# Nine elementwise instructions between SBUF tiles issued on GpSimd instead of VectorE, in a one-core attention and FFT kernel

## The chip, the cores and the metric

The kernel runs on one core of one Trainium2 chip. The metric is device time in microseconds (us) of one execution, the median of several runs. Five engines take part: TensorE (PE in the profile; its weight loads are PEld), VectorE (DVE), ScalarE (ACT), GpSimd (POOL) and SyncE (SP, which here only issues transfers). Each engine runs its own instructions strictly in the order in which they stand in the program, and waits on semaphores for the others.

## The reference

Two branches read the same input `x` (1 x 2048 x 448) and are mixed by a gate for each token:

```python
g = _sigmoid((x * gate_w).sum(-1, keepdims=True))
a = _A_ref(x, A_wqkv, A_wo)      # 16 heads of 28, softmax attention over 2048 tokens, output projection
b = _B_ref(x, B_w_r, B_w_i)      # irfft2(rfft2(x) * (w_r + 1j * w_i)) over tokens and channels
return g * a + (1 - g) * b
```

## The kernel before

**Attention.** Heads are worked on in four groups `g` of four (one head for each 32-partition strip), queries in four columns `c` of 512. That gives 16 group-column pairs, numbered `n`: the first eight are groups 0 and 1, the last eight groups 2 and 3. For each pair PE makes the scores of 16 key tiles (L500, `ps<-q,k`). The exponential of most key tiles is taken on ACT (L1111, into the ring buffer `ring`, 1024 columns at a time). For two to five key tiles of each pair it is approximated without ACT: DVE adds a constant to the scores, clamps them and writes them as 16-bit integers whose bits are a bf16 number (L1061, `pd<-ps`), and GpSimd makes three shifted copies of each such tile with one 64-bit integer addition a copy (L1075, `INT64_ADD pd<-pd`). The four versions of a tile, each with its own value weights `vd`, are summed on PE (L500, `pvb<-pd,vd`) together with the ACT tiles (`pvb<-ring,vw`). There are nine `pd` buffers, so GpSimd cannot write a copy before PE has read the one that lay in its buffer.

**Projections.** `proj_group` projects q and k of a group: DVE scales the product out of PSUM into `q` or `k` (L804), squares it (L809, `sq<-q` or `sq<-k`, four instructions of 128 x 512 for q of group 1), PE sums the squares (`ps<-sq,cst`), DVE copies the sums out (L826, `nrow`) and SP writes them as an extra row into `q` or `k`.

**Normalising.** At the end of each pair `n`, `normalise` copies the sums out of PSUM (L1241, `pvs`), sends the denominators through DRAM and back, broadcast (`rs`, `rr`, `Rb`), and multiplies `pvs` by `Rb` into `q` (L1253).

**FFT.** `background` runs the spectral branch between the attention's instructions: a transform over channels (16 steps `fwd`), over tokens (`fwd2`), then 16 steps `mid`, numbered `g`, which multiply the spectrum by the complex weights (L1437, products `t12` and `t34` out of PSUM), form the real and the imaginary part from them (L1442 subtracts, L1444 adds, both 128 x 225, SBUF to SBUF, into `Z`), and transform back on PE (`ps<-Z,CS`).

**Order.** Nothing is scheduled at run time. A table in the file (`TABLE`) gives the order in which every operation is emitted and the PSUM bank that it uses, so each engine's order is fixed by it. A DVE instruction that is marked `lk=True` goes through `ported`: the GpSimd instruction that follows it in the emitted order is given a wait for it (`self.port` in `pin`), so that the two do not run side by side. The squares, the multiplication of `normalise` and both `Z` instructions are so marked.

Of the kernel before, what the change touches and what calls it, by code (L numbers as in the profile page):

```python
# [19 lines left out]
ALU = mybir.AluOpType  # L20
# [123 lines left out]
def rows_of(ap, row0, stride, count, dims, offset=0):  # L144
    pitch = ap.ap[0][0]
    return _AP(tensor=ap.tensor, offset=ap.offset + row0 * pitch + offset,
               ap=[[pitch * stride, count]] + [list(d) for d in dims])
# [10 lines left out]
def dv(n, rate=1):  # L158
    return 0.067 + n / 960.0 / rate
# [145 lines left out]
class Kernel:  # L305
# [54 lines left out]
    def passed(self, ins):  # L360
        o = self.sc.op_now
        if o is None:
            return
        if o.eng == "PE":
            self.npe += 1
            for d in o.deps:
                if d.name == "dexp":
                    for p in d.all:
                        self.taken.setdefault(p.name, self.npe)
            o.at = self.npe  # L370
        elif o.name in ("dp1", "dexp"):
            o.at = max([d.at for d in o.deps if d.eng == "PE" or d.name == "dp1"])
            if self.copies:
                self.tc.declare_no_dep(ins, group="dexp", reason="product done",
                                       keep=[p for p in self.copies if self.taken.get(p.name, o.at) >= o.at])
            if o.name == "dexp":
                self.tc.add_to_no_dep_group("dexp", ins)
                self.copies.append(ins)
        o.all.append(ins)
# [409 lines left out]
    def proj_group(self, w, g, blocks, due, rel):  # L789
        self.sc.ctx = ("proj_group", w, g, tuple(blocks))  # L790
        nc = self.nc
        T = (self.k if w == "k" else self.q)[g]
        e2s, e1s = [], []
        prev = list(self.sqmm)
        nb = len(blocks)
        for j, b in enumerate(blocks):
            it = Item()
            dd = due - 8 + 5.0 * (j + 1) / nb
            m = self.proj_mms(w, g, b, it, dd, rel)
            dst = T[:, 512 * b:512 * b + 512]  # L800
            sqs = self.sq[:, 512 * b:512 * b + 512]

            def f1(dst=dst, it=it):
                self.pin(nc.vector.tensor_scalar(out=dst, in0=self.bgi(it), scalar1=SQ, scalar2=None,  # L804
                                                 op0=ALU.mult))
            e1 = self.dve(dv(512), f1, (m, ("kwar", g) if w == "k" else None), dd - 1.5, free=it)

            def f2(dst=dst, sqs=sqs):
                self.pin(nc.vector.tensor_tensor(out=sqs, in0=dst, in1=dst, op=ALU.mult))  # L809
            e2s.append(self.dve(dv(512, 2), f2, [e1] + prev, dd, lk=True))  # L810
            e1s.append(e1)
        it = Item()
        ms = []

        def f3():
            for j, b in enumerate(blocks):
                self.mm(self.bgi(it)[32 * j:32 * j + 32, :], self.c("sel4"), self.sq[:, 512 * b:512 * b + 512],
                        True, True, tile_position=(0, 32 * j))
        ms.append(self.pe(512, f3, e2s + [self.d_cst2], due - 3, mode="col", acq=it))
        self.sqall = getattr(self, "sqall", []) + ms  # L820
        self.sqmm = self.sqmm[:2] + [ms[-1]]
        self.nrow_i = getattr(self, "nrow_i", -1) + 1
        nr = self.nrow[self.nrow_i % 2]

        def f4():
            self.pin(nc.vector.tensor_copy(out=nr[0:32 * nb, :], in_=self.bgi(it)[0:32 * nb, :]))  # L826
        users = self.__dict__.setdefault("nrow_u%d" % (self.nrow_i % 2), [])
        ev = self.dve(dv(512), f4, [ms[-1]] + users, due - 3, free=it)
        row = 1 if w == "k" else 0
        ds = []  # L830
        for j, b in enumerate(blocks):
            def o(b=b):
                return rows_of(T[:], row, 32, 4, [[1, 512]], 512 * b)

            def i(j=j):
                return rows_of(nr[:], 32 * j, 1, 4, [[1, 512]])
            ds.append(self.dma(o, i, [ev] + e1s + e2s, due - 2.5, dur=0.55, lat=2.2))
        for b in blocks:
            (self.kev if w == "k" else self.qev)[g, b] = ds + e1s
        users[:] = ds  # L840
        if w == "k":
            self.knr[g, blocks[0]] = (nr, ev, users)
# [354 lines left out]
    def normalise(self, n, last):  # L1197
        self.sc.ctx = ("normalise", n)
        nc, sc = self.nc, self.sc
        g, c = self.groups[n]  # L1200
        i = n % 2
# [3 lines left out]
        pvs, rs, rr = self.pvs[i], self.rs[i], self.rr[i]  # L1205
        dst = self.q[g][:, 512 * c:512 * c + 512]
        if n == 15:
            kk = -50.0
# [31 lines left out]
        kk = t0 + 4  # L1240
# [7 lines left out]
        def bc(s):  # L1248
            src = sc_[:]
            return _AP(tensor=src.tensor, offset=src.offset + 512 * s, ap=[[0, 32], [1, 512]])  # L1250
        ds = [self.dma(lambda s=s: self.Rb[32 * s:32 * s + 32, :], lambda s=s: bc(s), (d2, self.rblast), kk, lat=2.5)
              for s in range(4)]
        e = self.dve(dv(512), lambda: self.pin(nc.vector.tensor_tensor(out=dst, in0=pvs[:], in1=self.Rb[:], op=ALU.mult)),  # L1253
                     ds, kk, lk=True)
        self.nlast[i] = self.rblast = e
        self.onorm[g, c] = e
        if g == 3:
# [73 lines left out]
    def background(self):  # L1331
        nc, sc = self.nc, self.sc
# [11 lines left out]
        def due(c):  # L1344
            return t_a + (t_b - t_a) * c / total
# [56 lines left out]
        pr, prw, prz, prt = [None, None], [None, None], [[], []], [None, None]  # L1402
# [6 lines left out]
        for g in range(NT):  # L1409
            i = g % 2  # L1410
            sc.ctx = ("mid", g)
            cost += 1.63
            k = due(cost)
            Wg, t12, t34, Z, CS = self.Wg[i], self.t12[i], self.t34[i], self.Z[i], self.CSt[i]
# [21 lines left out]
            def prod(out, it, Wg, off):  # L1436
                self.pin(nc.vector.tensor_tensor(out=out[:], in0=self.bgi(it)[:, 0:F2].rearrange("p (a f) -> p a f", a=2),  # L1437
                                                 in1=free_dims(Wg[:], [[F, 2], [1, F]], off), op=ALU.mult))
            o1 = self.dve(.54, lambda a=(t12, it, Wg, F): prod(*a), ops[-1:] + dl[1:] + prz[i], k)
            o2 = self.dve(.54, lambda a=(t34, it, Wg, 0): prod(*a), [o1] + prz[i], k, free=it)  # L1440
            prw[i] = o2
            z1 = self.dve(dv(225, 2), lambda t12=t12, Z=Z: self.pin(nc.vector.tensor_tensor(  # L1442
                out=Z[:, 0, :], in0=t12[:, 0, :], in1=t12[:, 1, :], op=ALU.subtract)), [o1, prt[i]], k, lk=True)
            z2 = self.dve(dv(225, 2), lambda t34=t34, Z=Z: self.pin(nc.vector.tensor_tensor(  # L1444
                out=Z[:, 1, :], in0=t34[:, 0, :], in1=t34[:, 1, :], op=ALU.add)), [o2, prt[i]], k, lk=True)
            prz[i] = [z1, z2]
            it2 = Item()
            ops2 = []
# [28 lines left out]
        for t in range(NT):  # L1477
            sc.ctx = ("inv", t)
            cost += .61
            k = due(cost)  # L1480
            v2 = self.V2[t % 3]
            d = self.dma(lambda v2=v2: v2[:], lambda t=t: rows_of(self.UT[:], 32 * (t >> 2) + (t & 3), 4, 8,
                                                                  [[F4, NT], [1, F4]]), vev + [v2r[t % 3]], k - 4, lat=3.5)
# [62 lines left out]
```

## Time and profile before

| | |
|---|---|
| Median of 3 runs | 380.87 us (379.72 to 381.80) |
| The profiled execution, its own time | 380.92 us |
| Its span, first to last instruction | 379.0 us |
| DVE busy | 336.6 us (89%) in 649 instructions |

The span is the part of the execution between the first and the last instruction of the program, so 1.9 us of the execution lie around it. Busy times of different engines overlap and do not add up to the span. A group's row gives the line in the program, the engine, the operation, the tiles written and read with their shapes, the count, then busy time, the mean of one in ns, and the engine's idle time just before these instructions, with what ended it. The granted TensorE clock was full throughout (0.999 of it as the mean).

### The profile page before, as it was taken

To read this page: it belongs to the slowest core of one execution; us is meant where nothing else is said; L and a number is where in the kernel's file an instruction comes from. 1 tells how busy PE (TensorE), PEld (TensorE's weight loads), DVE (VectorE), ACT (ScalarE), POOL (GpSimd) and SP (SyncE) were. 2 spreads that over 40 slices of the span, in tenths; PEclk is the share of its full clock that TensorE was granted. 3 is DMA by queue.
4 is the path that set the end of the run, shared out by engine and by line. 5 is a ranking of instruction groups with operands and counts; after the bars stand their busy time and mean duration, and the time that the engine had idled before them with its cause. 6 is when DMAs were issued, how large, how long until landed. Compare 5 with 4: busy or idle time off the path is not lost.

```text
span 379.0 us, 12133 instructions
## 1 busy us (share of the span) xinstructions
PE 367.8 (97%) x5093; PEld 144.0 (38%) x5093; DVE 336.6 (89%) x649; ACT 350.6 (92%) x389; POOL 234.9 (62%) x264
## 2 busy tenths in 40 slices
PE   8999999999999999999999999999999989999995
PEld 5644233343333332334334434233333333433563
DVE  1769889999999999999999999999999989996644
ACT  2799999999999999999989999999999999999741
POOL 4707295747878876483463556877877759654610
PEclk9999999999999999999999999999999999999999
DMA  6601001001201122113211212212313222222122
GB/s 145 171 3 45 3 5 47 21 6 39 60 15 31 47 57 52 51 38 99 68 38 39 70 36 73 59 39 64 80 41 80 66 48 80 70 67 72 48 78 88
DMA packets 31154, 21.20 MB, mean 56 GB/s; under 512 B 16260, under 2 KB 29052, under 8 KB 31100
## 3 DMA queue, kind: packets, MB, share of 16 engines
q1 hardware_dynamic: 29708, 19.96, 20.0%
q8 instruction: 40, 0.66, 0.7%
q10 hardware_dynamic: 1392, 0.46, 0.5%
q14 instruction: 14, 0.11, 0.1%
HBM read 14.51 MB, written 1.96 MB: 43 GB/s over the span
## 4 chain that ended last, share of the span: by engine, by line
PE 49%; ACT 41%; DVE 5%; SPq 1%; issue 1%; DMA 1%; POOL 0%; DVEq 0%; POOLq 0%
ACT ring L1111 41%; PE ps L500 32%; PE pvb L500 16%; DVE pd L1061 3%; SPq L475 1%; PE ps L503 1%; DMA out_dram<-wpk 1%; DVE X L1373 0%; DVE pvs L1241 0%; DVE t L1437 0%; DMA Wg<-in_B_w_r_dram 0%; ACT V L1321 0%; DVE wpq L1299 0%; DVE wpk L1299 0%; DVE Ab L1390 0%
## 5 line engine op out<-in xcount | busy, mean ns | idle before, releaser
L1111 ACT ACTIVATE ring<-ps 128x1024 bf16<-128x1024 f32 x374 | 345.6, 1135 | 7.3 <-PE ps L500 7.1
L1075 POOL INT64_ADD pd<-pd x207 | 213.0, 1044 | 107.2 <-DVE pd L1061 32.3
L1061 DVE TENSOR_SCALAR pd<-ps 128x512 uint16<-128x512 f32 x260 | 177.2, 715 | 6.1 <-PE ps L500 3.8
L500 PE MATMUL ps<-q,k 32*128 32x512 bf16 x1024 | 143.7, 382 | 4.3 <-ACT ring L1111 1.5
L500 PE MATMUL pvb<-pd,vd 128*32 128x512 bf16 x1104 | 94.8, 384 | 0.0
L500 PEld LDWEIGHTS <-k 32*128 32x128 bf16 x1024 | 40.9, 91 | 118.1 <-issue 113.2
L500 PE MATMUL pvb<-ring,vw 128*32 128x512 bf16 x748 | 68.8, 384 | 0.4 <-DVE pvs L1241 0.4
L500 PEld LDWEIGHTS <-vd 128*32 128x32 bf16 x1104 | 24.3, 95 | 33.1 <-issue 27.8
L500 PEld LDWEIGHTS <-vw 128*32 128x32 bf16 x748 | 17.5, 94 | 25.3 <-issue 22.4
L500 PEld LDWEIGHTS <-xT 128*128 128x128 bf16 (+5 forms) x512 | 19.4, 97 | 10.8 <-issue 9.9
L1437 DVE TENSOR_TENSOR t<-ps,Wg 128x450 bf16<-128x450 f32 x32 | 19.0, 619 | 1.5 <-PE pvb L500 1.0
L500 PE MATMUL ps<-xT,wpq 128*32 128x512 bf16 (+3 forms) x248 | 19.4, 382 | 0.3 <-DVE wpq L590 0.3
L500 PE MATMUL ps<-xT,wpk 128*32 128x512 bf16 (+3 forms) x244 | 18.4, 383 | 0.0
L1373 DVE TENSOR_TENSOR X<-ps,oc 128x226 bf16<-128x226 f32 (+1 forms) x32 | 12.2, 385 | 0.6
L500 PE MATMUL ps<-wvr,xT 128*128 128x112 bf16 (+1 forms) x192 | 12.7, 213 | 0.0
L500 PEld LDWEIGHTS <-CS 128*32 128x32 bf16 x384 | 8.8, 95 | 9.5 <-issue 5.2
L804 DVE TENSOR_SCALAR q<-ps 128x512 bf16<-128x512 f32 x15 | 10.3, 684 | 2.3 <-PE ps L500 2.3
L500 PE MATMUL ps<-wpk,q 128*32 128x448 bf16 x128 | 11.7, 362 | 0.0
L500 PE MATMUL ps<-wpq,q 128*32 128x448 bf16 x128 | 11.5, 362 | 0.0
L500 PE MATMUL ps<-Bd,xT 128*32 128x226 bf16 (+2 forms) x256 | 11.1, 263 | 0.3 <-ACT ring L1111 0.3
L1494 DVE TENSOR_TENSOR X<-ps,ogb 113x512 bf16<-113x512 f32 x16 | 10.3, 674 | 1.2 <-PE ps L500 1.2
L804 DVE TENSOR_SCALAR k<-ps 128x512 bf16<-128x512 f32 x15 | 10.3, 684 | 0.9 <-PE ps L500 0.8
(99 smaller groups left out, 270.5 us busy)
## 6 DMA issues: line engine op xcount, KB each, us to landing
Rb<-rsc SPq DMA_DIRECT2D x60, 64.0 KB
CS<-cCS SPq DMA_DIRECT2D x16, 192.0 KB
V<-xtok SPq DMA_DIRECT2D x16, 113.0 KB
Wg<-in_B_w_i_dram SPq DMA_DIRECT2D x64, 28.1 KB
xtok<-Ab SPq DMA_DIRECT2D x16, 112.5 KB
xtok<-in_A_x_dram SPq DMA_DIRECT2D x3, 448.0 KB
Wg<-in_B_w_r_dram SPq DMA_DIRECT2D x32, 28.1 KB
out_dram<-wpq SPq DMA_DIRECT2D x6, 112.0 KB
```

Of the source, the lines that this page charges most:

```text
L475: self.pin(e.dma_start(out=out() if callable(out) else out, in_=in_() if callable(in_) else in_))
L500: self.pin(self.nc.tensor.matmul(out, lhsT=lhsT, rhs=rhs, start=start, stop=stop, **kw))
L503: self.pin(self.nc.tensor.transpose(out=out, in_=in_, identity=self.c("ident")[0:n, 0:n]))
L804: self.pin(nc.vector.tensor_scalar(out=dst, in0=self.bgi(it), scalar1=SQ, scalar2=None, op0=ALU.mult))
L1061: self.pin(nc.vector.tensor_scalar(out=free_dims(ys[:], [[512 * e, w], [1, 512]], 512 * part[0]).bitcast(U16), in0=self.ps[:, bs[0]:bs[0] ...
L1075: self.pin(nc.gpsimd.int64_add(out=fl(pds), in0=fl(ys), in1=PHASE[f] * 0x0001000100010001))
L1111: self.pin(nc.scalar.activation(out=self.ring[:, u0:u0 + len(st), :], in_=self.ps[:, bs[0]:bs[0] + len(st), :], func=ACT.Exp, scale=LN2 / ...
L1373: self.pin(nc.vector.tensor_tensor(out=free_dims(self.X1[:, t, :], [[F, 2], [-1 if dif else 1, n]], (F - 1) * dif), in0=free_dims(self.bgi ...
L1437: self.pin(nc.vector.tensor_tensor(out=out[:], in0=self.bgi(it)[:, 0:F2].rearrange("p (a f) -> p a f", a=2), in1=free_dims(Wg[:], [[F, 2], ...
L1494: self.pin(nc.vector.tensor_tensor(out=free_dims(self.zt[0:FN], [[128, 4], [1, 128]], 512 * t), in0=self.bgi(it)[0:FN, :].rearrange("p (a ...
```

## The change

Nine instructions move from DVE to GpSimd (`nc.vector.tensor_tensor` becomes `nc.gpsimd.tensor_tensor`), at the same place of the emitted order: the four squares of q of group 1, the multiplication in `normalise` of the pair n = 3, and the subtraction and addition of the `mid` steps 5 and 6. As GpSimd instructions they are not marked `lk`. One line of bookkeeping in `passed` keeps a dependency on the instruction just before on the same engine. No loop, table entry, bank or tile changes.

```diff
@@ passed
-                                       keep=[p for p in self.copies if self.taken.get(p.name, o.at) >= o.at])
+                                       keep=[p for p in self.copies
+                                             if p is self.before.get(ins.engine) or self.taken.get(p.name, o.at) >= o.at])
@@ proj_group
-                self.pin(nc.vector.tensor_tensor(out=sqs, in0=dst, in1=dst, op=ALU.mult))
-            e2s.append(self.dve(dv(512, 2), f2, [e1] + prev, dd, lk=True))
+                e = nc.gpsimd if (w, g) == ("q", 1) else nc.vector
+                self.pin(e.tensor_tensor(out=sqs, in0=dst, in1=dst, op=ALU.mult))
+            e2s.append(self.pool(0.6, f2, [e1] + prev, dd) if (w, g) == ("q", 1) else
+                       self.dve(dv(512, 2), f2, [e1] + prev, dd, lk=True))
@@ normalise
+        if n == 3:
+            e = self.pool(0.9, lambda: self.pin(nc.gpsimd.tensor_tensor(out=dst, in0=pvs[:], in1=self.Rb[:], op=ALU.mult)),
+                          ds, kk)
+        else:
...
@@ background
+            ze, zn = (nc.gpsimd, lambda d, f, p: self.pool(d, f, p, k)) if g in (5, 6) else \
+                (nc.vector, lambda d, f, p: self.dve(d, f, p, k, lk=True))
+            z1 = zn(dv(225, 2), lambda t12=t12, Z=Z, ze=ze: self.pin(ze.tensor_tensor(
+                out=Z[:, 0, :], in0=t12[:, 0, :], in1=t12[:, 1, :], op=ALU.subtract)), [o1, prt[i]])
+            z2 = zn(dv(225, 2), lambda t34=t34, Z=Z, ze=ze: self.pin(ze.tensor_tensor(
+                out=Z[:, 1, :], in0=t34[:, 0, :], in1=t34[:, 1, :], op=ALU.add)), [o2, prt[i]])
```

The order in which the instructions of GpSimd stand around the squares, before. A row that begins with `L1075 ISA pd` is one `INT64_ADD`; the number behind a name is that of the buffer, and the brackets name the semaphores that the instruction waits for:

```order
L888 COPY vt<-w_89 128x20 [waits DVE_49,Activation_49]
L1075 ISA pd_110<-pd_108 128x1024
L1075 ISA pd_108<-pd_107 128x1024 [waits DVE_49,Pool_49]
L1075 ISA pd_105<-pd_103 128x1024
L1075 ISA pd_109<-pd_107 128x1024 [waits PE_49]
L1075 ISA pd_110<-pd_107 128x1024 [waits PE_49]
L1075 ISA pd_105<-pd_111 128x1024 [waits DVE_49,PE_49]
```

The same place of the change (its line numbers are a few higher: L1078 for L1075, L811 for L809):

```order
L811 ISA
L811 TENSOR_TENSOR sq<-q_81 128x512
L811 TENSOR_TENSOR sq<-q_81 128x512 [waits DVE_49] x2
L891 COPY vt<-w_89 128x20 [waits Activation_49]
L1078 ISA
L1078 ISA pd_110<-pd_108 128x1024
L1078 ISA pd_108<-pd_107 128x1024 [waits DVE_49,Pool_49]
L1078 ISA pd_105<-pd_103 128x1024
L1078 ISA pd_109<-pd_107 128x1024 [waits PE_49]
L1078 ISA pd_110<-pd_107 128x1024 [waits PE_49]
L811 ISA
L811 TENSOR_TENSOR sq<-q_81 128x512 [waits DVE_49]
```

The next row is again an `ISA` without operands, and then the additions go on. Such a row loads another library of GpSimd programs (it is a `PseudoReloadLibraryIndex` in the built program): index 0 ahead of a `TENSOR_TENSOR`, index 1 ahead of an `INT64_ADD`, since the two operations are in different libraries. The program before has one such row in all, ahead of its first `INT64_ADD`; the change has eleven. So what moved here is four squares and, with them, four library changes; and the wait of the `vt` copy for DVE is gone.

Further on in GpSimd's order, around the `Z` instructions of the `mid` steps 5 and 6, before:

```order
L1075 ISA pd_109<-pd_107 128x1024 [waits PE_49]
L1075 ISA pd_108<-pd_106 128x1024 [waits DVE_49,PE_49]
L888 COPY vt<-w_91 128x20
L1075 ISA pd_104<-pd_111 128x1024 [waits DVE_49]
L1075 ISA pd_105<-pd_111 128x1024
L1075 ISA pd_103<-pd_111 128x1024 [waits PE_49]
L1075 ISA pd_109<-pd_106 128x1024 [waits PE_49]
L1075 ISA pd_107<-pd_106 128x1024
L1075 ISA pd_104<-pd_110 128x1024 [waits DVE_49,PE_49]
```

The same place of the change, up to the second pair of `Z`:

```order
L1078 ISA pd_109<-pd_107 128x1024 [waits PE_49]
L1453 ISA
L1453 TENSOR_TENSOR Z_145<-t_143 128x225 [waits DVE_49]
L1451 TENSOR_TENSOR Z_145<-t_141 128x225 [waits DVE_49]
L1078 ISA
L1078 ISA pd_108<-pd_106 128x1024 [waits PE_49]
L891 COPY vt<-w_91 128x20
L1078 ISA pd_104<-pd_111 128x1024 [waits DVE_49]
L1078 ISA pd_105<-pd_111 128x1024
L1078 ISA pd_103<-pd_111 128x1024 [waits PE_49]
L1078 ISA pd_109<-pd_106 128x1024 [waits PE_49]
L1078 ISA pd_107<-pd_106 128x1024
```

Behind the last of these rows, ahead of `pd_104<-pd_110`, stands the second pair of `Z`, again between two library changes. The multiplication of `normalise` stands alone in the same way, with a change on both sides: it comes behind the third memset of an output weight (L728), ahead of `pd_111<-pd_109`. That makes five places with two library changes each. On DVE the nine rows are gone and nothing else moves; the orders of PE, ACT and SP are the same as before, with some of their waits turned from DVE to GpSimd.

More of the change, by code (lines that the diff above doesn't have):

```diff
@@ L1252, in normalise @@
               for s in range(4)]
-        e = self.dve(dv(512), lambda: self.pin(nc.vector.tensor_tensor(out=dst, in0=pvs[:], in1=self.Rb[:], op=ALU.mult)),
-                     ds, kk, lk=True)
+        if n == 3:
+            e = self.pool(0.9, lambda: self.pin(nc.gpsimd.tensor_tensor(out=dst, in0=pvs[:], in1=self.Rb[:], op=ALU.mult)),
+                          ds, kk)
+        else:
+            e = self.dve(dv(512), lambda: self.pin(nc.vector.tensor_tensor(out=dst, in0=pvs[:], in1=self.Rb[:], op=ALU.mult)),
+                         ds, kk, lk=True)
         self.nlast[i] = self.rblast = e
@@ L1441, in background @@
             prw[i] = o2
[L1442 to L1445, printed above, removed]
+            ze, zn = (nc.gpsimd, lambda d, f, p: self.pool(d, f, p, k)) if g in (5, 6) else \
[4 more added lines that the diff above has]
+                out=Z[:, 1, :], in0=t34[:, 0, :], in1=t34[:, 1, :], op=ALU.add)), [o2, prt[i]])
             prz[i] = [z1, z2]
```

## The prediction

> **What bounds the kernel now.** I read the page's busy times first, then the chain of work that ended last, then the timelines of ACT and of POOL.
>
> ```profile
> PE 367.8 (97%) x5093; PEld 144.0 (38%) x5093; DVE 336.6 (89%) x649; ACT 350.6 (92%) x389; POOL 234.9 (62%) x264
> PE 49%; ACT 41%; DVE 5%; SPq 1%; issue 1%; DMA 1%; POOL 0%; DVEq 0%; POOLq 0%
> ```
>
> The chain is made of PE and ACT; DVE, which the change relieves, holds 5% of it. POOL, which takes the work, has 38% of the span idle and no part in the chain. The shares are averages, so the places have to be looked at. ACT in order of time (start, duration, then what; the bracket is idle time just before):
>
> ```profile
> 82.13 81.10 ACT L1111 ACTIVATE ring<-ps 128x1024 bf16<-128x1024 f32 x88
> 163.41 5.61 ACT L1111 ACTIVATE ring<-ps 128x1024 bf16<-128x1024 f32 x6 [0.18 <-PE ps L500]
> 169.30 1.94 ACT L1111 ACTIVATE ring<-ps 128x1024 bf16<-128x1024 f32 x2 [0.28 <-PE ps L500]
> ...
> 185.39 8.36 ACT L1111 ACTIVATE ring<-ps 128x1024 bf16<-128x1024 f32 x9 [0.17 <-PE ps L500]
> 194.29 1.94 ACT L1111 ACTIVATE ring<-ps 128x1024 bf16<-128x1024 f32 x2 [0.55 <-PE ps L500]
> 196.87 4.82 ACT L1111 ACTIVATE ring<-ps 128x1024 bf16<-128x1024 f32 x5 [0.64 <-PE ps L500]
> ...
> 201.84 109.24 ACT L1111 ACTIVATE ring<-ps 128x1024 bf16<-128x1024 f32 x119
> 311.37 39.70 ACT L1111 ACTIVATE ring<-ps 128x1024 bf16<-128x1024 f32 x43 [0.29 <-PE ps L500]
> ```
>
> From 82 us to 351 us ACT does exponentials one behind the other. Its marked gaps there are 0.18 + 0.28 + 0.17 + 0.55 + 0.64 + 0.29 = 2.1 us. Whatever DVE is spared in this stretch, no more than these 2.1 us can come out of it; and every microsecond for which ACT is made to stand still is added to the end.
>
> PE is as full, as five stretches around the changed places show (the columns are the stretch and its length, then the busy time of PE, PEld, DVE, ACT and POOL, each with its count of instructions, the clock, DMA share and GB/s):
>
> ```profile
> 80.00:90.00 10.00, 9.72 (x143) 4.49 (x140) 8.96 (x21) 10.00 (x13) 7.03 (x8) 1.00 0.16 37
> 90.00:100.00 10.00, 10.00 (x145) 3.13 (x142) 9.96 (x19) 10.00 (x12) 8.65 (x9) 1.00 0.10 28
> 140.00:150.00 10.00, 10.00 (x154) 3.16 (x142) 9.95 (x23) 10.00 (x12) 7.13 (x9) 1.00 0.17 43
> 220.00:230.00 10.00, 9.44 (x121) 3.15 (x122) 9.75 (x23) 10.00 (x12) 6.02 (x9) 1.00 0.27 66
> 230.00:240.00 10.00, 9.73 (x134) 4.05 (x132) 9.52 (x19) 10.00 (x12) 5.65 (x6) 1.00 0.22 54
> ```
>
> All three big engines are full there; POOL alone has room, 1.4 to 4.4 us in 10. The kernel now runs because POOL's copies are always ready: PE reads 1104 / 4 = 276 of them and never waited (0.0 us idle).
>
> ```profile
> L500 PE MATMUL pvb<-pd,vd 128*32 128x512 bf16 x1104 | 94.8, 384 | 0.0
> ```
>
> **What is removed.** On DVE nine instructions go, by their means in ns:
>
> ```profile
> L809 DVE TENSOR_TENSOR sq<-q 128x512 bf16<-128x512 bf16 x15 | 5.9, 415 | 0.0
> L1253 DVE TENSOR_TENSOR q<-pvs,Rb 128x512 bf16<-128x512 f32 x15 | 10.8, 718 | 0.0
> L1442 DVE TENSOR_TENSOR Z<-t 128x225 bf16<-128x225 bf16 x16 | 4.4, 272 | 0.0
> L1444 DVE TENSOR_TENSOR Z<-t 128x225 bf16<-128x225 bf16 x16 | 4.3, 269 | 0.0
> ```
>
> 4 x 0.415 + 0.718 + 2 x 0.272 + 2 x 0.269 = 3.5 us of DVE. They lie at 84 to 93, at 144 and at 223 to 237 us, where ACT has no gap. I count this as 0 us; ACT hides it, and if that cover were gone, 2.1 us is the most. POOL's waits for these instructions go as well; what is late next is its own work.
>
> **What is added: the work itself.** No row of before shows a `TENSOR_TENSOR` on POOL. The nearest are these:
>
> ```profile
> L1075 POOL INT64_ADD pd<-pd x207 | 213.0, 1044 | 107.2 <-DVE pd L1061 32.3 <-PE pvb L500 22.8 <-DVE sq L809 18.1
> L576 POOL MEMSET wpk<- 128x512 bf16 x4 | 2.1, 533 | 0.1
> L590 POOL COPY wpq<-X 128x224 bf16<-128x224 bf16 x3 | 1.1, 372 | 0.8 <-DMA X<-in_A_wqkv_dram 0.8
> ```
>
> A memset of 512 elements takes 0.53 us and reads nothing: the lower bound. An `INT64_ADD` writes 512 words of 64 bits in 1.04 us; twice that, 2.1 us, since there are two operands, is the upper bound. I take 1.04 us for 512 elements, the row that is nearest in kind, and 0.5 us for 225: 5 x 1.04 + 4 x 0.5 = 7.2 us of POOL. The Trainium skill (GPSIMD Engine Reference, section 3.1) has 4497 ns for 2048 fp32 elements, by which 512 would be an estimated 1.1 us; no run here shows it.
>
> **What is added: ten library changes.** The one change that before contains stands ahead of the first addition, at line L1075, as a pair of MODIFY_POOL_CONFIG:
>
> ```profile
> L1075 POOLq MODIFY_POOL_CONFIG  x2: 1/1/1, 32.3 to 32.3; - x2
> 34.08 6.30 POOL L1075 INT64_ADD pd<-pd  x6 [1.80 <-DVE pd L1061]
> ```
>
> From 32.3 to 34.08 us, 1.8 us, is all that this change can have taken, and DVE was waited for in it anyway: bounds of 0 and 1.8 us for this one. But every earlier execution of this program had left the same library in place, and I do not know whether it was loaded again. After the change two libraries alternate, so code has to be brought each time. What bringing code costs is seen in the engines' instruction fetches:
>
> ```profile
> q8 instruction: 40, 0.66, 0.7%
> q14 instruction: 14, 0.11, 0.1%
> ```
>
> Queue 8 brings 0.66 MB / 40 = 16.5 KB a packet, in 0.7% x 379.0 x 16 / 40 = 1.06 us. Queue 14 brings 0.11 MB in 0.1% x 379.0 x 16 = 6.1 us of packet time. A library's size is in no row. One block, 1.06 us, is the near end, an image like that of queue 14, 6.1 us, the far one (7.1 us at queue 8's rate: 0.11 / 0.0165 = 6.7 blocks of 1.06 us). A library is a whole set of programs rather than one block, so I take **6.1 us** a change, both ways, as an estimate from these rows.
>
> The Trainium skill (GPSIMD Engine Reference, section 2.1) says that the first call to a freshly loaded kernel pays a load of about 6 us, measured as 5.95 us, that no instruction in the profile shows. The row at 32.3 us disagrees, unless the library was still there. By 5.95 us for every change the sum below would be 1.5 us smaller; by that row for both ways it is the rival of cheap changes.
>
> **The sum, place by place.** POOL's own timeline at the five places:
>
> ```profile
> 79.69 4.08 POOL L1075 INT64_ADD pd<-pd  x4 [5.62 <-PE pvb L500]
> 86.53 0.22 POOL L888 COPY vt<-w 128x20 f32<-128x20 f32 x1 [2.76 <-DVE sq L809]
> 86.70 5.50 POOL L1075 INT64_ADD pd<-pd  x5
> 93.33 8.25 POOL L1075 INT64_ADD pd<-pd  x8 [1.13 <-PE ps L500]
> ...
> 144.86 2.05 POOL L1075 INT64_ADD pd<-pd  x2 [1.39 <-PE pvb L500]
> 148.39 4.08 POOL L1075 INT64_ADD pd<-pd  x4 [1.49 <-DVE pd L1061]
> ...
> 226.60 1.04 POOL L1075 INT64_ADD pd<-pd  x1 [3.98 <-DVE Z L1442]
> ...
> 237.62 6.13 POOL L1075 INT64_ADD pd<-pd  x6 [4.35 <-DVE pd L1061]
> ```
>
> At each place POOL now does a change, the work and a change, 12.2 us plus the work, and what it can set against that is the idle time that it had there:
>
> - three squares: 12.2 + 3.1 - 2.76 = 12.5
> - the fourth square: 12.2 + 1.0 - 1.13 = 12.1
> - the multiplication of n = 3: 12.2 + 1.0 - 1.39 - 1.49 = 10.3
> - the first `Z` pair: 12.2 + 1.0 - 3.98 = 9.2
> - the second: 12.2 + 1.0 - 4.35 = 8.9
>
> Together 53.0 us. Behind the changes stand the next additions, in strict order; PE's sums over `pd` wait for these, the scores behind them in PE's queue wait too, and then ACT, which has no gap to lose. PE also waits for the squares directly (`ps<-sq,cst`), and SP's two `q` row transfers and one `Rb` transfer queue behind the same work. What would soften it is a lead of the copies over PE: nine buffers at one read each 1.2 us (276 in some 326 us) are at most 11 us, once, and at 79.69 POOL had just waited 5.6 us for a free buffer, so the copies were ahead there. I count 0 for the lead, bounded by those 11 us. Against the profiled execution's 380.9 us (379.0 span and 1.9 around it), practically the median of 380.87, this gives 380.9 + 53.0 = 433.9; I say **433 us**.
>
> **Rivals.**
>
> One way only: the change to library 1 costs at most the 1.8 us of the row at 32.3, and only the one to library 0 costs 6.1 us. For it speaks that this row was really measured; against it, that it may have found its library in place. Each place then has 7.9 instead of 12.2 us: 53.0 - 5 x 4.3 = 31.5, that is 412 us; with a free way back 22.5 us, 403 us.
>
> Cheap changes: both ways 1.8 us. The five places give 3.9, 3.5, 1.7, 0.6 and 0.3 us, 10 us together: 391 us.
>
> No cost: both libraries stay in the cores' memory and a change only turns a pointer. Then only the work counts against idle time of 15.1 us; the three squares exceed theirs by 0.4 us, the rest fits, and it is 381 us, no slower. This decides as soon as a change costs less than about 0.4 us (4 x 0.4 + 0.3 = 1.9 us at the two places of the squares). For it: the row's lower bound is 0. Against it: the built program has a load ahead of every change of operation, and code that is not there has to come from somewhere.
>
> Faster: with free changes, DVE's 3.5 us let PE start scores earlier where ACT has gaps; all the gaps are 2.1 us, so 379 us at best. The gaps lie at 163 to 201 and at 311 us, none at a changed place, which speaks against it.
>
> Dearer: 10 us a change while transfers run beside it would give 53.0 + 10 x 3.9 = 92 us, 473 us; no row has such a load.
>
> **How the numbers follow.** Forecast 0.52; one way 0.28; cheap 0.07; no cost 0.05; faster 0.02; dearer 0.06. The range reaches from the free way back (402) to 7.1 us a change with the work at its upper bound (53.0 + 10 + 5.2 + 2.0 = 70 us, 451), and a little beyond for refilling PE and ACT, one 0.9 us exponential at each place: 456 us. Outside lie cheap, no cost, faster and dearer, 0.20. By about 0.5%, 1.9 us, which is what a measurement of this kernel can tell from no change: slower 0.93, same 0.05, faster 0.02.
>
> **What would show it.** The changed profile should have 22 MODIFY_POOL_CONFIG, and POOL idle of about 6 us behind each pair, which no other engine's end explains, ten times. PE should now wait for POOL's `pd` and ACT for PE around 90, 160, 250 us. DVE's busy time falls by 3.5 us and buys nothing. A `TENSOR_TENSOR` of 512 on POOL should take 1.0 us. I am wrong if POOL's idle times at the five places stay below 4 us, or if those ahead of `TENSOR_TENSOR` and of `INT64_ADD` differ strongly (one way), or if PE does not wait for POOL.

## The result, and the profile after

The changed kernel takes 444.49 us (median of 4 runs, 441.39 to 446.18) where the kernel before took 380.96 in the same rounds: 1.166 times as long, with an interval of 1.159 to 1.174. 433 us was forecast, with a range of 402 to 456. A later measurement in more rounds gave 444.1 us and 1.166 (1.163 to 1.169).

The profiled execution took 445.22 us, 443.4 of it span. From its page, the busy times, the granted clock in 40 slices and the shares of the chain that ended last:

```profile
PE 383.3 (86%) x5093; PEld 145.7 (33%) x5093; DVE 337.3 (76%) x640; ACT 353.4 (80%) x389; POOL 242.5 (55%) x273
PEclk9999999965599999589999997865999999999999
PE 48%; ACT 27%; issue 9%; POOL 5%; DMA 5%; DVE 4%; SPq 2%; ACTq 0%; DVEq 0%; POOLq 0%
```

Three things are new. PE and ACT are no longer full: 97% and 92% have become 86% and 80%. The chain now has 9% of "issue", 40 us in which an engine stood still and no other engine's end explains it. And the clock of TensorE, 9 in every slice before, falls at three places.

The library changes are the pairs of MODIFY_POOL_CONFIG, by line (the answers for the five lines that have them; count, duration in ns, first and last start):

```profile
L811 POOLq MODIFY_POOL_CONFIG  x4: 10/10/11, 83.7 to 105.0; - x4
L1257 POOLq MODIFY_POOL_CONFIG  x2: 10/10/10, 170.1 to 170.1; - x2
L1451 POOLq MODIFY_POOL_CONFIG  x2: 6/6/6, 284.3 to 284.4; - x2
L1453 POOLq MODIFY_POOL_CONFIG  x2: 9/9/9, 263.5 to 263.5; - x2
L1078 POOLq MODIFY_POOL_CONFIG  x12: 1/1/1, 32.2 to 292.8; - x12
```

They are 22, and 11 ns long at most. What they cost stands in the row of the instruction behind them. POOL's timeline, the rows of the moved instructions and of the first addition behind each:

```profile
90.62 3.03 POOL L811 TENSOR_TENSOR sq<-q 128x512 bf16<-128x512 bf16 x3 [6.86 <-DVE pd L1064]
...
99.75 5.21 POOL L1078 INT64_ADD pd<-pd  x5 [5.93 <-issue]
112.03 1.03 POOL L811 TENSOR_TENSOR sq<-q 128x512 bf16<-128x512 bf16 x1 [7.07 <-issue]
118.90 5.22 POOL L1078 INT64_ADD pd<-pd  x5 [5.84 <-issue]
...
177.27 1.25 POOL L1257 TENSOR_TENSOR q<-pvs,Rb 128x512 bf16<-128x512 f32 x1 [7.20 <-issue]
184.82 6.11 POOL L1078 INT64_ADD pd<-pd  x6 [6.29 <-issue]
...
270.76 0.56 POOL L1453 TENSOR_TENSOR Z<-t 128x225 bf16<-128x225 bf16 x1 [7.32 <-issue]
271.29 0.56 POOL L1451 TENSOR_TENSOR Z<-t 128x225 bf16<-128x225 bf16 x1
277.67 1.03 POOL L1078 INT64_ADD pd<-pd  x1 [5.81 <-PE ps L501]
...
291.49 0.56 POOL L1451 TENSOR_TENSOR Z<-t 128x225 bf16<-128x225 bf16 x1 [7.17 <-issue]
292.02 0.56 POOL L1453 TENSOR_TENSOR Z<-t 128x225 bf16<-128x225 bf16 x1
298.32 6.11 POOL L1078 INT64_ADD pd<-pd  x6 [5.74 <-issue]
```

The brackets are to be read here: ahead of each `TENSOR_TENSOR` POOL is idle for 6.9 to 7.3 us (mean 7.1), ahead of each first addition behind one for 5.7 to 6.3 us (mean 5.9). That makes 65.2 us in ten gaps, and the work itself 7.5 us. Two of the gaps name a releaser, because another instruction happened to end in them; their length is that of the others.

The groups of PE and ACT that wait, from the page (busy time and mean ns, then the idle time ahead of them and what ended most of it):

```profile
L501 PE MATMUL pvb<-pd,vd 128*32 128x512 bf16 x1104 | 99.0, 399 | 40.6 <-POOL pd L1078 40.5
L1114 ACT ACTIVATE ring<-ps 128x1024 bf16<-128x1024 f32 x374 | 348.4, 1118 | 69.7 <-PE ps L501 69.3
```

The second group's row in the profile of before:

```profile
L1111 ACT ACTIVATE ring<-ps 128x1024 bf16<-128x1024 f32 x374 | 345.6, 1135 | 7.3 <-PE ps L500 7.1
```

PE waits 40.5 us for POOL's copies, where it never waited before, and ACT 69.3 us for PE's scores instead of 7.1. That ACT's wait grew by 62 us is nearly the whole loss. It is more than PE's waits for POOL make: 40.5 us for copies, and 5.5 and 3.6 us for squares and `Z` by the gaps ahead of these, 49.6 in all. Stretches of the last place show what comes on top (stretch, length, busy time of PE, PEld, DVE, ACT and POOL with their instructions, granted clock, DMA share, GB/s):

```profile
287.80:291.00 3.20, 0.00 (x0) 0.00 (x0) 0.56 (x1) 1.36 (x2) 0.00 (x0) 1.00 0.27 47
291.00:299.40 8.40, 0.00 (x0) 0.00 (x0) 0.00 (x0) 0.00 (x0) 2.17 (x4) 0.50 0.09 27
299.40:311.40 12.00, 12.00 (x93) 2.51 (x92) 7.81 (x12) 7.61 (x8) 9.40 (x10) 0.50 0.07 18
311.60:340.00 28.40, 27.73 (x349) 8.73 (x345) 27.53 (x57) 28.17 (x32) 20.10 (x20) 1.00 0.25 57
```

At the last place PE stops at 287.8 us; 3.2 us later the granted clock falls to 0.50. PE starts again at 299.4 us and is full for 12 us, but at half the clock: 93 recorded matmuls in 12 us, 7.8 per us, against 349 in 28.4, 12.3 per us, behind. ACT, which was full before, is busy for 7.61 of these 12 us. So a stall of PE has a tail, which no term of the predicted sum has. The theory to test: the ten changes are the cost, through POOL's copies, PE and ACT, and the clock adds to it. The rivals: the work on POOL, or its new waits, cost much of it; or the low clock costs nothing, since POOL sets the pace.

### The profile page after: what moved, and what is told of

Read it like the earlier page. It is cut to its first block, busy times and chain, and to the rows that moved or that the text cites. A ratio compares the mean times of both kernels' runs of the same rounds, so it can differ in the third digit from the quotient of the medians.

```text
span 443.4 us, 12157 instructions
## 1 busy us (share of the span) xinstructions
PE 383.3 (86%) x5093; PEld 145.7 (33%) x5093; DVE 337.3 (76%) x640; ACT 353.4 (80%) x389; POOL 242.5 (55%) x273
## 2 busy tenths in 40 slices
DMA packets 31155, 21.20 MB, mean 48 GB/s; under 512 B 16260, under 2 KB 29052, under 8 KB 31100
## 4 chain that ended last, share of the span: by engine, by line
PE 48%; ACT 27%; issue 9%; POOL 5%; DMA 5%; DVE 4%; SPq 2%; ACTq 0%; DVEq 0%; POOLq 0%
PE ps L501 30%; ACT ring L1114 27%; PE pvb L501 17%; POOL pd L1078 3%; SPq L476 2%; DVE pd L1064 2%; DMA out_dram<-wpk 2%; DMA xtok<-in_A_x_dram 2%; POOL sq L811 1%; DMA X<-in_A_wqkv_dram 1%; PE ps L504 1%; DMA xtok<-Ab 1%; DVE pvs L1244 0%; DMA Wg<-in_B_w_r_dram 0%; DVE wpq L1306 0%
## 5 line engine op out<-in xcount | busy, mean ns | idle before, releaser
L1114 ACT ACTIVATE ring<-ps 128x1024 bf16<-128x1024 f32 x374 | 348.4, 1118 | 69.7 <-PE ps L501 69.3
L1078 POOL INT64_ADD pd<-pd x207 | 213.2, 1045 | 130.5 <-DVE pd L1064 30.2
L501 PE MATMUL ps<-q,k 32*128 32x512 bf16 x1024 | 148.3, 398 | 2.7 <-ACT ring L1114 0.9
L501 PE MATMUL pvb<-pd,vd 128*32 128x512 bf16 x1104 | 99.0, 399 | 40.6 <-POOL pd L1078 40.5
L501 PE MATMUL pvb<-ring,vw 128*32 128x512 bf16 x748 | 72.0, 402 | 0.4 <-DVE pvs L1244 0.4
L501 PEld LDWEIGHTS <-xT 128*128 128x128 bf16 (+5 forms) x512 | 20.6, 100 | 11.6 <-issue 10.8
L501 PE MATMUL ps<-Z,CS 128*32 128x225 bf16 (+1 forms) x192 | 10.6, 314 | 3.8 <-POOL Z L1451 3.6
L501 PE MATMUL ps<-wvr,xT 128*128 128x112 bf16 (+1 forms) x192 | 13.9, 228 | 0.0
L829 DVE CAST nrow<-ps 32x512 bf16<-32x512 f32 (+1 forms) x12 | 8.2, 682 | 6.9 <-PE ps L501 6.6
L1380 DVE TENSOR_TENSOR X<-ps,oc 128x226 bf16<-128x226 f32 (+1 forms) x32 | 12.3, 385 | 0.6
L1244 DVE COPY pvs<-pvb 128x512 f32<-128x512 f32 x15 | 10.3, 689 | 3.1 <-PE pvb L501 2.6
L805 DVE TENSOR_SCALAR q<-ps 128x512 bf16<-128x512 f32 x15 | 10.3, 686 | 2.4 <-PE ps L501 2.4
```

The lines of the kernel that those rows point to most:

```text
L501: self.pin(self.nc.tensor.matmul(out, lhsT=lhsT, rhs=rhs, start=start, stop=stop, **kw))
L1078: self.pin(nc.gpsimd.int64_add(out=fl(pds), in0=fl(ys), in1=PHASE[f] * 0x0001000100010001))
L1114: self.pin(nc.scalar.activation(out=self.ring[:, u0:u0 + len(st), :], in_=self.ps[:, bs[0]:bs[0] + len(st), :], func=ACT.Exp, scale=LN2 / ...
L1244: ev = self.dve(0.61, lambda: self.pin(nc.vector.tensor_copy(out=pvs[:], in_=self.pv[:])), last + [self.nlast[i]], -100.0)
L1380: self.pin(nc.vector.tensor_tensor(out=free_dims(self.X1[:, t, :], [[F, 2], [-1 if dif else 1, n]], (F - 1) * dif), in0=free_dims(self.bgi ...
```

## The experiments

**Copies in place of the products.** The moved instructions stay on GpSimd, but do an operation that needs no other library (the four lines alike; the copy in place of the multiplication reads `pvs` and not `Rb`):

```diff
-                self.pin(e.tensor_tensor(out=sqs, in0=dst, in1=dst, op=ALU.mult))
+                self.pin(e.tensor_copy(out=sqs, in_=dst) if (w, g) == ("q", 1) else
+                         e.tensor_tensor(out=sqs, in0=dst, in1=dst, op=ALU.mult))
```

> The changed kernel, with the nine operations on GpSimd replaced by plain copies (tensor_copy) that write the same tiles at the same places; so it leaves out squaring q of group 1, the multiplication by Rb for n = 3, and the difference and sum of Z in steps 5 and 6. A copy like this stands between additions in the kernel before already without a library change, so 2 changes in the program are left of 22. Theory (the library changes are the cost, the work itself fits into POOL's idle time): 381 us, within 1% of the kernel before; no POOL idle of 6 to 7 us at the five places. Rival A (the cost is the work on POOL, its place in POOL's row or its sharing with DVE): above 390 us. Rival B (relieving DVE of 3.5 us is worth something when no library changes come with it): 377 to 379 us.

Measured: 379.01 us against 380.78, 0.9958 of it (0.9943 to 0.9973). POOL's timeline at the squares:

```profile
83.22 1.87 POOL L811 COPY sq<-q 128x512 bf16<-128x512 bf16 x3
85.04 0.21 POOL L892 COPY vt<-w 128x20 f32<-128x20 f32 x1
85.22 1.03 POOL L1079 INT64_ADD pd<-pd  x1
...
91.58 0.61 POOL L811 COPY sq<-q 128x512 bf16<-128x512 bf16 x1
92.17 5.21 POOL L1079 INT64_ADD pd<-pd  x5
```

No bracket, no gap. (The 22 and the 2 of the expectation are MODIFY_POOL_CONFIG; two of them make one change.) With nine instructions on POOL at the same places of its order, the kernel is not slower. So the place and the sharing cost nothing that can be measured. What this run does not cover: a copy of 512 elements takes 0.61 us, a product 1.03, and the copy for n = 3 does not need `Rb`. The 379.01 us lie 2 us under the theory's 381, at the upper edge of rival B: DVE is spared 3.5 us and the end comes 1.0 to 2.2 us earlier. For these nine instructions that is about the most that the idea can bring.

**The changes without the work.** The kernel before with all nine operations on DVE, and a tiny product on GpSimd at the same places:

```diff
+    def tiny(self):
+        self.tc.keep_in_program_order(self.nc.gpsimd.tensor_tensor(
+            out=self.small[:], in0=self.zero[:, 0:8], in1=self.zero[:, 0:8], op=ALU.mult))
...
+                if (w, g) == ("q", 1):
+                    self.tiny()
```

> The kernel before, all nine operations still on DVE, plus seven products of 128 x 8 elements on GpSimd (small<-zero, three at the first place and one at each other), whose result nobody reads. So the ten library changes come without the work and without any new wait between DVE and POOL. Theory (changes of 7.1 and 5.8 us stop POOL's copies, PE runs dry and its clock falls with it): 430 to 442 us, POOL idle of 6.9 to 7.3 us ahead of the tiny products and 5.5 to 6.3 us ahead of the additions behind them, PE waiting for pd. Rival A (the work, or the waits of PE and DVE for it, make up most of the 63 us): below 400 us.

Measured: 438.36 us, 1.152 (1.148 to 1.155). POOL's timeline at the squares:

```profile
91.17 0.75 POOL L382 TENSOR_TENSOR small<-zero 128x8 bf16<-128x8 bf16 x3 [7.41 <-issue]
91.86 0.22 POOL L895 COPY vt<-w 128x20 f32<-128x20 f32 x1
97.77 5.20 POOL L1082 INT64_ADD pd<-pd  x5 [5.68 <-issue]
109.85 0.19 POOL L382 TENSOR_TENSOR small<-zero 128x8 bf16<-128x8 bf16 x1 [6.88 <-issue]
116.25 5.21 POOL L1082 INT64_ADD pd<-pd  x5 [6.21 <-issue]
```

0.94 us of products here bring the same gaps as 4.06 us in the changed kernel. The changes alone cost 438.4 - 380.8 = 57.6 us, of the 63.5 us that the whole change costs. The other 5.9 us were not taken apart; the products are 6.0 us shorter here (1.5 us instead of 7.5). Together with the first run this settles what costs: the library changes.

**Which operations bring them.** A different kind of work moved to GpSimd, eight scalings with one input:

```diff
-                    self.pin(nc.vector.tensor_scalar(
+                    self.pin((nc.gpsimd if f > 1 else nc.vector).tensor_scalar(
                         out=free_dims(self.vd[g][:], [[32, n4], [1, DH + 1]], 128 * (DKT * f + o4)),
...
+                rd.append(self.pool(0.7, fs, dep, due - 1.3) if f > 1 else
```

> The kernel before, with another kind of work moved: 8 of the 16 scalings vd<-vt (TENSOR_SCALAR, one input from SBUF, 0.5 us each on DVE) on GpSimd, at five places between the additions. Question: is it the product of two tiles (TENSOR_TENSOR) that needs the other library, or any arithmetic? Theory A (TENSOR_SCALAR lies in the library of TENSOR_TENSOR, so it brings ten changes too): POOL idle of about 7 us ahead of these and 5.8 us behind, 420 to 445 us. Theory B (it is at home like a copy): 379 to 383 us and 2 changes in the program.

Measured: 445.27 us, 1.171 (1.166 to 1.176). One of the five places:

```profile
121.68 1.70 POOL L950 TENSOR_SCALAR vd<-vt 128x580 bf16<-128x580 f32 x1 [7.47 <-issue]
129.34 4.08 POOL L1077 INT64_ADD pd<-pd  x4 [5.96 <-issue]
```

Theory A holds: `TENSOR_SCALAR` brings the same two gaps at five places, with 22 MODIFY_POOL_CONFIG in all (the time is just above the 420 to 445 us that were expected; these scalings take 13.7 us of POOL). In this kernel copies, casts and memsets stand between the additions without a change; products and scalings do not.

**Why the one change in before was cheap.** The prediction could not say whether 1.8 us was the price of a change or that of finding the library in place. The tiny product of the run above, now only as the last instruction of the program, leaves the other library behind:

```diff
+        self.tiny()
```

> The kernel before plus one tiny product on GpSimd (small<-zero) as the last instruction of the program, so that the next execution begins with the other library in place. Question: was the change ahead of the first addition in the kernel before (at most 1.8 us) cheap because its library had been left in place by the execution before, or because a change there costs little anyway? Theory A (left in place): the first addition now starts at about 38 us instead of 34.0. Theory B (cheap at this place, e.g. its load was asked for early): it starts at 34.0 as before. The time by either: 381 us plus 0 to 9 us, since the change at the end may itself hold the end up by up to 7 us.

Measured: 382.58 us, 1.005 (1.004 to 1.007). POOL's timeline at the first addition and at the end:

```profile
37.76 6.89 POOL L1081 INT64_ADD pd<-pd  x6 [6.11 <-DVE glog L921]
...
370.50 0.38 POOL L382 TENSOR_TENSOR small<-zero 128x8 bf16<-128x8 bf16 x1 [7.01 <-issue]
```

The first addition now begins at 37.76 us instead of 34.08, behind a gap of 6.11 us: theory A. An execution begins with the library that the one before left, and the row of 1.8 us in the profile of before showed a change that had nothing to load. Both changes here lie where little waits for POOL, and cost 1.8 us together.

**One place alone.** The changed kernel with only the multiplication of n = 3 on GpSimd:

```diff
-                e = nc.gpsimd if (w, g) == ("q", 1) else nc.vector
+                e = nc.gpsimd if False else nc.vector
...
-            ze, zn = (nc.gpsimd, lambda d, f, p: self.pool(d, f, p, k)) if g in (5, 6) else \
+            ze, zn = (nc.gpsimd, lambda d, f, p: self.pool(d, f, p, k)) if False else \
```

> The changed kernel with only one of its five places: the multiplication of n = 3 on GpSimd, the squares and Z back on DVE. 4 library changes in the program. Theory (each pair of changes costs 7.1 + 5.8 us of POOL, and the places add up): 381 + 12 to 14 = 393 to 395 us, as the delay grew by 12.6 to 14.2 us at this place of the changed kernel. Rival (the first change in an execution is dear and later ones dearer or cheaper, or the five places disturb each other): below 388 or above 398 us.

Measured: 393.99 us against 379.96, 1.037 (1.033 to 1.041): 14.0 us for one pair of changes, as in the theory. (The profile has six MODIFY_POOL_CONFIG, that is three changes, one of them at the start, and not four.) So this place costs alone what it costs among the five, where ACT's row lost 14.2 us there; the other four were not run alone. ACT's timeline behind the stall:

```profile
161.65 1.02 ACT L1114 ACTIVATE ring<-ps 128x1024 bf16<-128x1024 f32 x1 [12.22 <-PE ps L501]
163.16 1.02 ACT L1114 ACTIVATE ring<-ps 128x1024 bf16<-128x1024 f32 x1 [0.49 <-PE ps L501]
164.59 1.02 ACT L1114 ACTIVATE ring<-ps 128x1024 bf16<-128x1024 f32 x1 [0.41 <-PE ps L501]
166.14 1.03 ACT L1114 ACTIVATE ring<-ps 128x1024 bf16<-128x1024 f32 x1 [0.52 <-PE ps L501]
167.68 10.34 ACT L1114 ACTIVATE ring<-ps 128x1024 bf16<-128x1024 f32 x11 [0.51 <-PE ps L501]
```

Behind the 12.22 us come four more gaps of 0.41 to 0.52 us, while the clock is half.

**The clock at this place.** The same kernel, with 11.6 us of matmuls of zeros added into `pvb` where PE waited for `pd`:

```diff
+    STALLS = [(1880, 11.6)]
+
+    def keep_busy(self, o):
+        if o.eng == "PE" and self.STALLS and self.npe - self.extra >= self.STALLS[0][0]:
+            n = int(self.STALLS.pop(0)[1] / self.EACH)
+            for _ in range(n):
+                self.filler(0 if self.pv_open else -1, 256)
```

> The kernel with the multiplication of n = 3 alone on GpSimd, plus 11.6 us of zero matmuls into pvb where PE waited 11.9 us for pd. One place, one wait, nothing behind it that could hide the clock. Theory (at this place the half clock costs the 1.7 to 2.3 us by which the delay grew from 12.5 us at the first exponential to 14.2 some exponentials later): 391.5 to 392.5 us where it was 394.0 without the fill, granted clock 1.0. Rival (it costs nothing): 394 us or more.

Measured: 390.98 us, 1.028 (1.025 to 1.030), with the granted clock at 1.000. ACT's timeline:

```profile
160.59 14.14 ACT L1126 ACTIVATE ring<-ps 128x1024 bf16<-128x1024 f32 x15 [11.11 <-PE ps L513]
```

The gaps behind the stall are gone: fifteen exponentials without one. PE does more, all of it useless, and the kernel is 3.0 us faster. So at a single place the half clock costs up to 3.0 us beside a stall of 11; the theory had 1.7 to 2.3. Not all of the 3.0 us need be the clock. In the two profiles the way back did not take the same time, so the first copy came 0.63 us later without the fill:

```profile
158.29 6.10 POOL L1078 INT64_ADD pd<-pd  x6 [6.74 <-issue]
157.66 6.11 POOL L1090 INT64_ADD pd<-pd  x6 [5.91 <-issue]
```

(The two were measured on two chips; the intervals of their ratios, 1.033 to 1.041 and 1.025 to 1.030, do not meet.)

**The clock at all places, in three fits.** The same fill at the stalls of the changed kernel, as a list of places (the number of the matmul) and lengths in us, and one more inside the sums of the squares:

```diff
-    STALLS = [(1880, 11.6)]
+    STALLS = [(1082, 11.5), (1137, 3.7), (1880, 11.9), (2991, 3.6), (3136, 11.6)]
...
+                if (w, g, j) == ("q", 1, 2):
+                    for i in range(2 * int(5.5 / self.EACH)):
```

> The changed kernel plus matmuls of zeros on PE at the places where it ran dry (adding zero to pvb, or writing a bank that is overwritten afterwards), about as long as its stalls: 11.5, 5.5, 3.7, 11.9, 3.6 and 11.6 us. POOL's row and its library changes stay. Theory (of the 63 us, about 15 are the TensorE clock, which was granted at 0.5 for 10 to 30 us behind each stall): mean granted clock 0.98 or more instead of 0.915, and 427 to 434 us. Rival (only the stalls cost; the low clock is hidden since ACT sets the pace): 444 us or, for matmuls that overrun the stalls, more, however the clock goes.

Measured: 439.79 us, 1.155 (1.152 to 1.158), clock 0.979. Neither: less than the theory's gain, and the fill did not fit. The one ahead of the last square ran from 106.5 to 117.7 us, where the changed kernel's stall had ended at 113.1. But one row led on. The wait for `pd` ahead of the second `Z` pair, in this run:

```profile
282.39 1.04 PE L513 MATMUL pvb<-pd,vd 128*32 128x512 bf16 x8 [5.23 <-POOL pd L1096]
```

and in the changed kernel:

```profile
283.17 0.61 PE L501 MATMUL pvb<-pd,vd 128*32 128x512 bf16 x8 [1.30 <-POOL pd L1078]
```

With the clock up, PE came to this wait earlier, and waited 5.23 us instead of 1.30 for a copy that came at much the same time. So at this place the slow clock had cost next to nothing. That made a second theory, with the fill fitted anew:

```diff
-    STALLS = [(1082, 11.5), (1137, 3.7), (1880, 11.9), (2991, 3.6), (3136, 11.6)]
+    STALLS = [(1082, 12.0), (1094, 0.9), (1137, 4.9), (1880, 11.8), (2991, 3.5), (3081, 5.1), (3136, 11.4)]
...
-                    for i in range(2 * int(5.5 / self.EACH)):
+                    for i in range(2 * int(7.6 / self.EACH)):
```

> The changed kernel with the zero matmuls fitted anew to its stalls at full clock (12.0, 0.9, 7.6, 4.9, 11.8, 3.5, 5.1 and 11.4 us), so that PE neither idles for long nor overruns. POOL's row and its library changes stay. First theory (the half clock costs about 15 us beside the stalls): 428 to 432 us. Second theory, formed on the first fill, where PE at full clock came to the next wait for POOL earlier and waited there for 5.2 instead of 1.3 us (most of the half clock lies in front of a wait for POOL that ends at the same time anyway; only what comes behind a place's last wait is paid, about 1 + 2 + 5 us): 434 to 438 us. Rival (the clock costs nothing): 443 us or more.

Measured: 443.43 us, 1.167 (1.165 to 1.169), though the clock was 0.999. By the numbers this is the rival's result, but the fill had overrun again:

```profile
106.13 14.81 PE L513 MATMUL ps<-zero 128*32 128x256 bf16 x268
```

It ends at 120.9 us; the last square, a POOL instruction of 1.03 us, began at 113.00 in this run. This overrun of 6.9 us was repaired:

```diff
-                    for i in range(2 * int(7.6 / self.EACH)):
+                    for i in range(67):
```

> As the second fill, with the one among the squares halved: its matmuls go to two row groups instead of four and took 0.055 us each, not 0.028, so that it ended at 120.9 us where the squares were ready at 114.0. Second theory (most of the half clock lies in front of a wait for POOL that ends at the same time anyway): 435 to 438 us, about 7 less than the second fill and than the changed kernel, with the clock at 1.0. First theory (15 us of clock): 428 to 432 us. Rival (the clock costs nothing): 442 us or more.

Measured: 436.9 us, 1.149 (1.146 to 1.153), the clock 1.000 in every stretch. To compare it on one chip and in the same rounds:

> The changed kernel as it is, on the same chip and in the same rounds as its version with the fitted zero matmuls, to size the part of the clock better than two runs on two chips do (444.5 and 436.9 us, with intervals of 1.5% and 0.7%). Expected: 443 to 446 us, and 6 to 9 us above that version, if the half clock costs about 7.6 us. Rival (the difference was that of two chips): less than 3 us.

> The changed kernel with the fitted zero matmuls, as in the third fill, beside the changed kernel on the same chip. Expected: 436 to 438 us.

Measured: 444.1 us for the changed kernel (1.1663, 1.1633 to 1.1693) and 436.93 with the fill (1.1468, 1.1448 to 1.1488). The half clock costs 7.2 us of the 63.2, if the fill itself costs nothing. (It fits to within about 0.5 us: in the first profile of this fill the part among the squares ended at 113.2 us, 0.4 us behind the last square.) The second theory holds. The first one, 15 us, took the growth of the span less the waits that PE shows; but a wait grows when PE arrives earlier.

The profile of this second measurement of the changed kernel also shows how much the tail varies. At the last place PE starts again at 300.76 us, and the clock is back after 5.5 us, where it took 12 us in the first profile:

```profile
300.70:306.20 5.50, 5.44 (x42) 1.16 (x45) 2.91 (x5) 2.83 (x3) 5.08 (x6) 0.50 0.01 3
306.30:330.00 23.70, 22.95 (x291) 7.29 (x283) 23.26 (x46) 23.50 (x27) 17.02 (x17) 1.00 0.19 46
```

ACT's row lost 14.1 us at this place there, and 15.9 us in the first profile.

## Why the prediction was right

**The bound** held. DVE's relief brought nothing in the changed kernel, and 1.8 us by the medians (1.0 to 2.2) where no changes came with it, about the 2.1 us that ACT's gaps allowed. One sign failed: DVE's busy time did not fall by 3.5 us (336.6 to 337.3). In part other work on it took longer (the scalings `vd<-vt` 9.2 us in all where they took 7.3); why was not tried.

**The work** was sized well: 1.03 us for a product of 512 elements against 1.04, 1.25 with an fp32 input, 0.56 against 0.5 for 225.

**The changes** were placed and counted right: ten, all dear, in both directions. The rival of one way only, with 0.28, rested on the row of 1.8 us. It fell with the gaps of 5.7 to 6.3 us ahead of the additions, and the run that left the other library behind showed why that row had been cheap. The price, 6.1 us, was near (7.1 and 5.9), but its derivation was not good: it read the size of a library off queue 14, by a share printed as 0.1%, which rounded could stand for anything from 3.0 to 9.1 us. In the changed kernel that queue has one packet more, queue 8 none, and the page of the profile counts 31155 DMA packets in all where there were 31154:

```profile
DMA packets 31155, 21.20 MB, mean 48 GB/s; under 512 B 16260, under 2 KB 29052, under 8 KB 31100
...
q8 instruction: 40, 0.66, 0.7%
q14 instruction: 15, 0.12, 0.1%
```

The run with the copies, which has one change in all, shows the same 15 packets on queue 14. So ten loads left no traffic in any queue shown, and that the estimate came out near was luck. The Trainium skill (GPSIMD Engine Reference, section 2.1) gives 5.95 us for such a load and says that no instruction shows it. The trace agrees with the second, and with the first for the way back (5.9 us); the way to `TENSOR_TENSOR` took 7.1 us.

**The sum** of 53.0 us was 10.2 us short of the 63.2 us that the later rounds give. Its form was right: with the measured terms in the same formula, 65.2 for the changes and 7.5 for the work less the 15.1 us of idle time, it gives 57.6 us, and the run at full clock has 436.9 - 380.9 = 56.0. So the 10.2 us are 4.6 for the sizes of the terms (4.2 of it the changes) and 7.2 for the clock, less the 1.6 by which the formula is above the run. By this balance the lead of the copies, counted as 0, was small. By place, as the lateness that ACT's row gained there (the same exponential, by its number in the row, in before and in the other kernel):

| place | predicted | changed kernel | with fill, clock 1.0 |
|---|---|---|---|
| four squares | 24.6 | 26.5 | 24.7 |
| n = 3 | 10.3 | 14.2 | 11.9 |
| first `Z` pair | 9.2 | 8.0 | 8.7 |
| second `Z` pair | 8.9 | 15.9 | 11.6 |

So the changes were mis-sized, the split between the two `Z` pairs was wrong, and one term was missing. A pair of changes is 13.0 us, not 12.2: 4.2 us in all. The second `Z` pair cost more than its term and the first less; at full clock the two together cost 20.3 us, and the formula with the measured terms gives 20.0. At the second, POOL's 4.35 us of idle time were no longer there to set against the changes. In the changed kernel its changes begin at 284.3 us, 6.6 us after the first pair's way back ended at 277.67, and POOL has no time to spare in between; that is read from the rows, not tried. Missing was the **clock**, 7.2 us: the last step of the prediction allowed one exponential per place for refilling PE and ACT, and that only at the edge of the range. The range held with 11 us to spare because its end had been opened for other reasons, to 7.1 us a change and to the upper bound of the work; that it covers the clock is in part luck.

The Trainium skill has a rule for this term (TensorE: Matmul & The Clock Gate, Terms): the loss is the throttled time by one minus the clock's share. The mean granted clock of 0.915 in 443.4 us is 75 us at half, which by that rule is an estimated 38 us. The runs show 7.2 us; the rule is far too high here. For 36 of the 75 us PE has nothing to do, by the gaps of its timeline, and of the rest much lies ahead of a wait for POOL that ends no sooner for a faster PE.

## What to carry to other kernels

Before work is moved to an engine with idle time, look at what the engine must load to do it: in this kernel a product of 0.19 us from another library brought 13 us of gaps with it, and of what was moved only copies came without a change. A price read off one cheap row holds only if that row had to do the whole job; the first change of a program that runs again and again did not. A stall of a full PE costs more than its length, because the clock falls behind it, but here that cost little ahead of a next wait that something else ended.

## What the runs showed of the hardware

- A library change of GpSimd was, in the changed kernel's profile, a gap of 6.9 to 7.3 us ahead of `TENSOR_TENSOR` and of 5.7 to 6.3 us ahead of `INT64_ADD`, each time, also for a library that had been in place 11 us before (the products end at 93.65 us, and the next change to theirs is issued at 105.0). Over the profiles of all runs the gaps were 6.6 to 7.7 us ahead of products and scalings and 5.7 to 6.7 us ahead of additions; the tiny products saw up to 7.6 us. Nothing in the profile marks it but two MODIFY_POOL_CONFIG of some ns and idle time put down to "issue". The library that is loaded outlives the execution.
- The clock of TensorE fell to 0.50 at 291.0 us, 3.2 us after PE had stopped, and stayed there until 311.4 us, 12 us after PE had started again and was full. In the other profile of the same kernel it was back after 5.5 us at this place. The Trainium skill (TensorE: Matmul & The Clock Gate, Part 1) has about 3.4 us for both ways; the first agrees, the second does not; why it took so long was not tried.
- Copies, casts and memsets of GpSimd stood between its `INT64_ADD` without a change of library; `TENSOR_TENSOR` and `TENSOR_SCALAR` brought one on each side. Of the kernels measured only the one with copies took less time than the kernel before (0.4% less), and it leaves the work out.
